# Twice as many softmax tiles turned by the DMA crossbar, v tiles kept, and small softmax operations written another way

## The chip, the cores and the metric

The kernel runs on 1 core of one Trainium2 chip. The metric is the device time of one execution in microseconds (us). Before the change three runs took 913.06, 915.95 and 915.98 us; the median is 915.95 us. The core has five instruction queues: PE (matrix products; its weight loads are listed as PEld), DVE, ACT and POOL (elementwise work), and SP, which in this kernel issues nearly all DMAs. Each queue runs its instructions in the order in which they were written into it; an instruction that waits holds back all that stand behind it on its queue.

## The reference

Eight batches of 576 tokens go through attention with 8 heads of 64 columns and then through a gated feed-forward layer. Scores below the row's maximum minus `tau` are left out of the softmax:

```python
scores = scale * np.matmul(q, k.transpose(0, 1, 3, 2))
thresh = np.max(scores, axis=-1, keepdims=True) - tau
scores = np.where(scores >= thresh, scores, -1000000000.0)
scores = scores - np.max(scores, axis=-1, keepdims=True)
attn = np.exp(scores)
attn = attn / (np.sum(attn, axis=-1, keepdims=True) + 1e-09)
attn_out = np.matmul(attn, v)
x = attn_out.transpose(0, 2, 1, 3).reshape(B, S, H * D)       # 8 x 576 x 512
h = np.maximum(x @ w_in, 0.0)                                 # 512 -> 1024
conv_out[:, s] = sum(conv_w[k] * hp[:, s + k] for k in (0, 1, 2))   # hp: h with a zero row at both ends
gate = 1.0 / (1.0 + np.exp(-conv_out))
out = h * gate @ w_out                                        # 1024 -> 512
```

## The kernel before

**Tiling.** Heads are handled two at a time; a batch has 4 such pairs of heads. The 576 query rows are five tiles: four of 128 rows and one of 64. A batch is cut into two chunks, tiles 0 and 1, and tiles 2, 3 and 4. A *pair* (numbered `i`, 64 in all) is one pair of heads in one chunk; a *unit* (numbered `u`, 160 in all) is one tile of one pair, with both heads. In a pair of even place `p` the tiles run upward, in one of odd place downward.

**One unit** (function `unit`, from line 552). For each head PE writes 128x576 scores into a PSUM buffer `ps_s` (two buffers; line 573 for batch 0, line 580 for the others). DVE takes the row's negative maximum (`top`, L588) into a column of a small tile `few`; ACT writes exp(score - maximum) into `em` (L597); the limit, maximum minus tau, is a small operation of its own for each head (L592 on ACT or L594 on DVE or POOL); DVE zeroes what lies below the limit and sums the row (`mask`, L600). Then, for both heads at once, a guard is added to the sums (L617), a second column is set to 1/576 in rows whose sum is zero (L621, the "empty row" operation), and the guarded sum is inverted (L624, DVE). POOL multiplies `em` by the inverse and adds that second column (`norm`, L633), 128x576 for each head.

**Turning a unit.** The product with `v` needs `em` with keys on the partitions. Mostly PE does that: nine 128x128 transposes of a full tile (L692), in two groups of four and one block that is turned with the pair's other tiles at the pair's end; ACT copies them from PSUM into `eT` (L687). From batch 1 on, the first full tile of a pair of even place goes another way (`crossed`, `cross`): ACT and POOL copy the upper and lower halfwords of `em` into `parts` (L326, L328), SP writes `parts` to a DRAM buffer `rows` (L665), and two transposing DMAs of the crossbar read that into `eT` (L670). `CROSS = (1, 0)` says: one tile in pairs of even place, none in those of odd place. That is 28 of 160 units.

**Attention product.** `attend` multiplies `eT` with `v` (L747, L756) for two pairs together, so it waits for both pairs' `eT`; ACT and DVE then write the chunk's activations `x`. `eT` has two buffers, one for each of the two pairs.

**Feed-forward.** `mm1` (L784, result `ph`) and `mm2` (L842, result `po`) of an earlier chunk are spread between the units. Between them stand `relu` into `hp` (L799), two taps (L806), tanh (L813), gate (L811) and the split into a high and a low part (L821, L333). `hp` gets a zero column at its left or right end by POOL (L794, L796).

**What sets the order.** `Plan.op` records every operation with an estimated duration; `Plan.run` is a list scheduler that walks through these estimates once, when the program is built, and thereby fixes each queue's order. For a DMA it keeps a clock of the transfers (`ring`) and adds `late` to what it believes the landing to take. Some operations may be put on another engine when their own has a backlog (`other=`).

## Time and profile before

| | before |
|---|---|
| runs shown | 913.06, 915.95, 915.98 us |
| span of the profiled execution | 910.8 us |
| PE busy | 874.6 us, 96% |
| DVE busy | 751.2 us, 82% |
| ACT busy | 673.8 us, 74% |
| POOL busy | 603.5 us, 66% |
| packets of the DMA queue that SP fills | 133.90 MB, 55.3% of 16 DMA engines |

The profile is one execution, seen by the hardware's own recorder. The span runs from the first to the last recorded instruction, 910.8 us; the median of the runs is 5.15 us above it. "Busy" is the time in which an engine had an instruction of the program in work. PE's matmuls overlap in its pipeline, so that the duration of one matmul is longer than the time after which the next one starts; where PE's work is priced, the distance from start to start is what counts.

### The profile page before, as it was taken

The page shows a single profiled execution, that of the slowest core. Times are in us where ns is not written, and L with a number is a line of the kernel's source. Part 1 is how long each engine was busy: PE and PEld are TensorE (multiplying, and loading weights), DVE is VectorE, ACT ScalarE, POOL GpSimd, SP SyncE. Part 2 cuts the span into 40 slices and gives each one's busy share as a digit, 9 for nine tenths or more (in the row PEclk, how much of TensorE's full clock was granted, in tenths as well). Part 3 has the DMA queues.
Part 4 walks back from the last instruction along what each step waited for, and adds up shares of the span by engine and source line. Part 5 has one row for each costly group of instructions (what it writes and reads, how often), then busy time and mean ns, then how long its engine had stood idle before and what let it go on. Part 6 is the DMA issues. An engine that isn't in the chain of part 4 may idle for free.

```text
span 910.8 us, 19147 instructions
## 1 busy us (share of the span) xinstructions
PE 874.6 (96%) x6056; PEld 708.6 (78%) x6056; DVE 751.2 (82%) x1871; ACT 673.8 (74%) x1459; POOL 603.5 (66%) x1027
## 2 busy tenths in 40 slices
PE   5978799999999999999999999999999999999998
PEld 3545577878878788888788797887888878887896
DVE  5988999988988689987889789996988779997542
ACT  4878687878777777777768687877867778776642
POOL 2656778875767677685767767776776758675322
PEclk9989899999999999999999999999999999999999
DMA  6555257667764667647665377557667276654000
GB/s 213 155 162 170 57 143 197 149 178 181 198 175 113 163 175 198 158 116 202 169 157 157 117 201 191 140 118 202 173 176 179 89 187 159 181 137 112 13 24 35
DMA packets 148260, 137.02 MB, mean 150 GB/s; under 512 B 85312, under 2 KB 116288, under 8 KB 148160
## 3 DMA queue, kind: packets, MB, share of 16 engines
q1 hardware_dynamic: 147296, 133.90, 55.3%
q10 hardware_dynamic: 864, 1.90, 0.6%
q8 instruction: 49, 0.80, 0.4%
q14 instruction: 51, 0.42, 0.2%
HBM read 58.88 MB, written 25.95 MB: 93 GB/s over the span
## 4 chain that ended last, share of the span: by engine, by line
PE 73%; ACT 8%; DVE 6%; POOL 5%; DMA 4%; issue 3%; SPq 2%; ACTq 0%; POOLq 0%; DVEq 0%
PE po L842 20%; PE ph L784 16%; PE pa L756 12%; PE ps_s L580 11%; PE ps_t L692 9%; PE ps_s L573 3%; ACT em L597 2%; POOL em L633 2%; DVE em L600 2%; ACT eT L687 2%; PE pa L747 2%; DVE few L588 2%; DMA q<-in_qd_dram 1%; SPq L513 1%; DMA q<-q 1%
## 5 line engine op out<-in xcount | busy, mean ns | idle before, releaser
L633 POOL TENSOR_SCALAR em<-em,few 128x576 f32<-128x576 f32 x287 | 262.8, 924 | 29.9 <-DVE few L624 22.1
L600 DVE SCALAR_TENSOR_TENSOR em<-ps_s,few,em 128x576 f32<-128x576 f32 x288 | 230.5, 812 | 25.4 <-ACT em L597 17.1
L588 DVE TENSOR_REDUCE few<-ps_s 128x1 f32<-128x576 f32 x288 | 211.5, 748 | 39.3 <-PE ps_s L573 22.0
L597 ACT ACTIVATE em<-ps_s,few 128x576 f32<-128x576 f32 x288 | 210.5, 741 | 35.8 <-DVE few L588 31.5
L784 PE MATMUL ph<-x,w1h 128*128 128x322 f32 (+1 forms) x1024 | 233.7, 304 | 0.6 <-ACT hp L799 0.5
L687 ACT ACTIVATE eT<-ps_t 128x512 f32<-128x512 f32 (+2 forms) x360 | 168.0, 487 | 24.5 <-PE ps_t L692 22.4
L784 PEld LDWEIGHTS ph<-x,w1h 128*128 128x128 f32 x1024 | 173.1, 189 | 4.7 <-issue 3.0
L692 PE MATMUL ps_t<-ident,em 128*128 128x128 f32 x1060 | 157.8, 280 | 6.5 <-POOL em L633 5.1
L580 PE MATMUL ps_s<-ks,q 128*128 128x288 f32 x896 | 156.8, 306 | 5.3 <-DMA q<-q 2.1
L784 PE MATMUL ph<-x,w1l 128*128 128x322 f32 (+1 forms) x512 | 151.3, 295 | 0.0
L692 PEld LDWEIGHTS ps_t<-ident,em 128*128 128x128 f32 x1060 | 126.5, 143 | 31.5 <-POOL em L633 14.9
L580 PEld LDWEIGHTS ps_s<-ks,q 128*128 128x128 f32 x896 | 129.2, 189 | 20.2 <-issue 8.2
L333 POOL TENSOR_TENSOR gl<-t,gh 128x255 fp32r<-128x255 f32 (+9 forms) x192 | 119.6, 637 | 28.5 <-ACT gh L821 27.5
L756 PE MATMUL pa<-eT,v 128*64 128x320 f32 (+1 forms) x1024 | 132.1, 410 | 0.0
L842 PE MATMUL po<-w2h,gh 128*128 128x512 f32 x288 | 117.9, 409 | 0.3 <-ACT hp L799 0.3
L756 PEld LDWEIGHTS pa<-eT,v 128*64 128x64 f32 x1024 | 70.4, 137 | 59.3 <-issue 15.8
L842 PE MATMUL po<-w2l,gh 128*128 128x512 f32 x288 | 113.3, 393 | 0.0
L842 PE MATMUL po<-w2h,gl 128*128 128x512 f32 x288 | 113.1, 393 | 0.1
L806 DVE SCALAR_TENSOR_TENSOR t<-hp,cr 128x321 f32<-128x321 f32 (+1 forms) x128 | 75.6, 594 | 28.0 <-ACT hp L799 28.0
L784 PEld LDWEIGHTS ph<-x,w1l 128*128 128x128 f32 x512 | 96.8, 189 | 0.2
L813 ACT ACTIVATE t<-t,cm 128x321 f32<-128x321 f32 (+1 forms) x128 | 68.0, 535 | 25.2 <-DVE t L806 12.2
L811 DVE SCALAR_TENSOR_TENSOR t<-t,hp 128x321 f32<-128x321 f32 (+1 forms) x128 | 73.1, 573 | 11.4 <-ACT t L813 9.8
(80 smaller groups left out, 1104.1 us busy)
## 6 DMA issues: line engine op xcount, KB each, us to landing
q<-q SPq DMA_DIRECT2D x336, 64.0 KB, 2.1
v<-in_vc_dram SPq DMA_DIRECT2D x64, 288.0 KB, 3.8
rows<-parts SPq DMA_DIRECT2D x28, 576.0 KB, 3.3
k<-in_kp_dram SPq DMA_DIRECT2D x35, 320.0 KB, 3.5
out_dram<-ot SPq DMA_DIRECT2D x36, 256.0 KB, 2.3
xk<-in_kt_dram SPq DMA_DIRECT2D x28, 288.0 KB, 3.4
ks<-xk SPq DMA_DIRECT2D x56, 144.0 KB, 3.3
xq<-in_qt_dram SPq DMA_DIRECT2D x56, 128.0 KB, 2.9
```

Source lines behind the costliest of these rows:

```text
L333: engines[e].tensor_tensor(dst, x, y, op=ALU.subtract)
L580: nc.tensor.matmul(ps[:, c, :CH], lhsT=q[:, h, o:o + n], rhs=k[:, h, c * CH:(c + 1) * CH], start=(i == 0), stop=(i == 1))
L588: nc.vector.tensor_reduce(few[:rows, nm], ps[:rows, :, :CH], op=ALU.max, axis=mybir.AxisListType.XY, negate=True)
L597: nc.scalar.activation(view(), ps[:rows, :, :CH], AF.Exp, bias=few[:rows, nm])
L600: nc.vector.scalar_tensor_tensor(view(), ps[:rows, :, :CH], few[:rows, th], view(), op0=ALU.is_ge, op1=ALU.mult, accum_out=few[:rows, total])
L633: engines[e].tensor_scalar(sl, sl, by, to, op0=ALU.mult, op1=ALU.add)
L687: "act", act(w, True), lambda dst=dst, src=src: nc.scalar.activation(dst(), src(pt), AF.Copy),
L692: nc.tensor.transpose(out=pt[:, at:at + P], in_=em[:, int(b * P):int(b * P) + P], identity=ident[:])
L756: nc.tensor.matmul(pa[j * D:(j + 1) * D, :w], lhsT=vt[:, blk, :], rhs=eT[:, :w // D, blk, :], start=False, stop=(r == 3))
L784: nc.tensor.matmul(ph[:, :an], lhsT=w1[w][:, cb, fs], rhs=xs[cb][:, h, :an], start=(cb == 0 and i == 0), stop=(cb == NCB - 1 and i == 2))
L806: nc.vector.scalar_tensor_tensor(t[:, :kn], hp[:, k:kn + k], cr[:, j, f:f + 1], y, op0=ALU.mult, op1=ALU.add)
L842: nc.tensor.matmul(po[:], lhsT=x[:, f, at:at + P], rhs=w[:, f, :], start=(f == 0 and i == 0), stop=(f == NFB - 1 and i == 2))
```

## The change

Seven things change, and with them the order on every queue.

- `CROSS` becomes `(1, 1)`: in pairs of odd place too, the first full tile goes by the crossbar. 56 units instead of 28.
- A pair of a batch's second chunk uses the `v` tile that the same heads loaded for the first chunk, from batch 1 on; there are four buffers for `v` instead of two. 36 loads instead of 64. `parts` has one buffer instead of two.
- `few` is four lasting tiles. They are filled once with a tiny number (2^-80 times 576), and two columns are set to `tau`, so that a maximum stands beside a `tau` and a sum beside the tiny number. The limits of both heads are then one DVE sum over pairs of columns (line 608 of the new kernel), and the guarded sums another (line 635). Both heads' masks come after that one limit.
- There is no empty-row operation. `norm` adds 2^-80 to each element and multiplies by the inverse: one column of `few` is read instead of two.
- `hp` is three lasting tiles whose zero columns are written once; the column that the first tap starts from is shifted instead.
- The limit and the guard can no longer go to POOL or ACT, and `norm` no longer to ACT.
- The planner's estimates of DMA times, of `norm` and of tanh are changed.

```diff
+LEAST = 2.0 ** -80
+FEW = 4
+VB = 4
-CROSS = (1, 0)
+CROSS = (1, 1)
...
-            self.tile = self.pool.tile(self.shape, self.dtype, tag=self.tag, bufs=self.bufs, name=self.name)
+            self.tile = self.home or self.pool.tile(self.shape, self.dtype, tag=self.tag, bufs=self.bufs, name=self.name)
...
+    fews = [const(f"few{i}", [P, 12], F32) for i in range(FEW)]
+    hps = [const(f"hp{i}", [P, CW + 2], F32) for i in range(HPB)]
+    for x in fews:
+        op("pool", 100, lambda x=x: nc.gpsimd.memset(x[:], LEAST * S), w=[(x, 0)], ahead=200.0)
+        op(
+            "dve", 150, lambda x=x: nc.vector.tensor_scalar(x[:, 1:4:2], x[:, 1:4:2], 0.0, tau_sb[:], op0=ALU.mult, op1=ALU.add),
+            w=[(x, 0)], r=[(tau_sb, 0)], ahead=100.0
+        )
+    for x in hps:
+        op("pool", 100, lambda x=x: nc.gpsimd.memset(x[:, 0:CW + 2:CW + 1], 0.0), w=[(x, 0)], ahead=5.0)
...
-        op(queue, issue, fn, ring=rows * (n * 0.225 + 4) * 0.0737, **kw)
+        op(queue, issue, fn, ring=rows * n * 0.0149, **kw)
...
-        vt = plan.buf(wk, "v", 2, [P, NBLK, D], F32, f"v_{i}")
+        if b and chunks[pairs[i][0]].new[0]:
+            return vts[i - NP]
+        vt = plan.buf(wk, "v", VB, [P, NBLK, D], F32, f"v_{i}")
...
+            def limit():
+                pairs = few[:rows, :2 * m].rearrange("p (h two) -> p h two", two=2)
+                nc.vector.tensor_reduce(few[:rows, 8:8 + m], pairs, negate=True, **add)
...
-            op("dve", 125, limit, w=[(few, ("th", h))], r=[(few, ("nm", h)), (ntau, 0)], ahead=a, other=[("pool", 260), ("act", 110)])
-            op("dve", 738, mask, w=[(em, h), (few, ("sum", h))], r=[(ps, 0), (few, ("th", h))], ahead=a)
+            late.append(mask)
+            if h == m - 1:
+                op("dve", 85, limit, w=[(few, "th")], r=[(few, ("nm", x)) for x in range(m)], ahead=a)
+        for h in range(m):
+            op("dve", 738, late[h], w=[(em, h), (few, ("sum", h))], r=[(pss[h], 0), (few, "th")], ahead=a)
...
-            engines[e].tensor_scalar(few[:rows, inverse], few[:rows, sums], 1e-9, 1.0, op0=ALU.add, op1=ALU.mult)
-        def even(e):
-            engines[e].tensor_scalar(few[:rows, shift], few[:rows, sums], 0.0, 1.0 / S, op0=ALU.is_equal, op1=ALU.mult)
+        def guard():
+            pairs = few[:rows, 4:4 + 2 * m].rearrange("p (h two) -> p h two", two=2)
+            nc.vector.tensor_reduce(few[:rows, inverse], pairs, **add)
...
-                    engines[e].tensor_scalar(sl, sl, by, to, op0=ALU.mult, op1=ALU.add)
+                engines[e].tensor_scalar(sl, sl, LEAST, few[:rows, 10 + h:11 + h], op0=ALU.add, op1=ALU.mult)
-            choice = {"pool": 807, "dve": 400, "act": 625}
+            choice = {"pool": 728, "dve": 400}
...
-        parts = plan.buf(wk, "parts", 2, [P, 2, 2 * S], U16, f"parts_{u}")
+        parts = plan.buf(wk, "parts", 1, [P, 2, 2 * S], U16, f"parts_{u}")
-            w=[(rows, 0)], r=[(parts, 0), (parts, 1)], ahead=a, late=-500
+            w=[(rows, 0)], r=[(parts, 0), (parts, 1)], ahead=a, late=350
-            op("sp", 1560, turn, w=[(eT, (off, j))], r=[(rows, 0)], ahead=a, late=100, ring=1785)
+            op("sp", 1560, turn, w=[(eT, (off, j))], r=[(rows, 0)], ahead=a, late=350, ring=1840)
...
-        def edge():
-            if o:
-                nc.gpsimd.memset(hp[:, 0:1], 0.0)
-            if k0 + kn == S:
-                nc.gpsimd.memset(hp[:, kn + 1:kn + 2], 0.0)
-            nc.scalar.activation(hp[:, o:o + an], ph[:, :an], AF.Relu, scale=0.5)
+            nc.scalar.activation(hp[:, 1:1 + an], ph[:, :an], AF.Relu, scale=0.5)
```

What the queues hold now is shown at three places around pairs 24 and 25, the first two pairs of batch 3 (units 60 and 61, and 62 and 63). In a name such as `ps_t_62_0_4515`, 62 is the unit, 0 the group of blocks, and the last number only counts what was written before.

**PE, the turning of pair 25.** Before, unit 62 is turned by two groups of four transposes, between feed-forward matmuls (`ph`):

```order
L784 MATMUL ph_4_6_4502<-x_16_3236,w1h_275 128x256
L784 MATMUL ph_4_6_4502<-x_17_3253,w1h_275 128x256
L784 MATMUL ph_4_6_4502<-x_17_3253,w1l_301 128x256
L784 MATMUL ph_4_6_4502<-x_17_3253,w1h_275 128x256
L692 MATMUL ps_t_62_0_4515<-ident_83,em_62_4309 128x128 x4
L692 MATMUL ps_t_62_4_4522<-ident_83,em_62_4309 128x128 x4
L784 MATMUL ph_4_6_4502<-x_18_3497,w1h_275 128x256
L784 MATMUL ph_4_6_4502<-x_18_3497,w1l_301 128x256
L784 MATMUL ph_4_6_4502<-x_18_3497,w1h_275 128x256
```

In the changed kernel no transpose of unit 62 is left; at the pair's end only unit 63 is turned, and its last block alone (before, that last group held a block of unit 62 as well):

```order
L701 MATMUL ps_t_63_0_4279<-ident_100,em_63_4186 128x128 x4
L701 MATMUL ps_t_63_4_4288<-ident_100,em_63_4186 128x128 x4
L845 MATMUL po_9_4250<-w2h_765,gh_1021 128x512
L845 MATMUL po_9_4250<-w2h_765,gl_1026 128x512
L845 MATMUL po_9_4250<-w2l_787,gh_1021 128x512
L701 MATMUL ps_t_63_8_4302<-ident_100,em_63_4186 128x128
```

Nine transposes are gone from this pair, and so from each of the 28 pairs of odd place from batch 1 on.

**PE, ahead of the attention product of pairs 24 and 25, in the changed kernel.** These rows stand between the second crossbar instruction that writes `eT` of pair 25 and the product that reads it (in the program's order over all queues):

```order
L596 MATMUL ps_s_66_0_4368<-ks_3_3_4063,q1_27_4169 128x288
L596 MATMUL ps_s_66_0_4368<-ks_3_3_4063,q2_27_4177 128x288
L596 MATMUL ps_s_66_0_4368<-ks_3_3_4063,q1_27_4169 128x288
L596 MATMUL ps_s_66_0_4368<-ks_3_3_4063,q2_27_4177 128x288
L596 MATMUL ps_s_66_1_4376<-ks_3_3_4063,q1_27_4169 128x288
L596 MATMUL ps_s_66_1_4376<-ks_3_3_4063,q2_27_4177 128x288
L596 MATMUL ps_s_66_1_4376<-ks_3_3_4063,q1_27_4169 128x288
L596 MATMUL ps_s_66_1_4376<-ks_3_3_4063,q2_27_4177 128x288
L756 MATMUL pa_24_4389<-eT_24_4153,v_24_3825 64x256 x2
L756 MATMUL pa_25_4392<-eT_25_4297,v_25_3865 64x256 x2
L765 MATMUL pa_24_4389<-eT_24_4153,v_24_3825 64x256 x8
L765 MATMUL pa_25_4392<-eT_25_4297,v_25_3865 64x256 x8
```

Eight score matmuls of unit 66 are all that PE is given there.

**SP, the crossbar of pairs 24 and 25.** Before, one pair goes by the crossbar, and both load `v` (`q1`, `q2` and `ks` are operands of the scores, moved between partitions; `xq` and `k` are loads):

```order
L513 DMA q1_27_4375<-q1_27_4375 64x256
L513 DMA q2_26_4377<-q2_26_4377 64x256
L549 DMA v_24_4447<-in_vc_dram 128x576
L670 DMA_TRANSPOSE eT_24_4457<-rows_60_4299 128x9x128 x2
L549 DMA v_25_4507<-in_vc_dram 128x576
L513 DMA ks_3_3_4369<-xk_3_3_4245 64x576
L513 DMA q1_27_4375<-q1_27_4375 64x256
L513 DMA q2_27_4437<-q2_27_4437 64x256 x2
L538 DMA xq_28_4567<-in_qt_dram 128x256
L492 DMA k_28_4579<-in_kp_dram 128x640
```

Now a second write of `rows` and a second pair of transposing DMAs stand within the next dozen issues; the loads of `v` that remain are those of the first chunk's pairs (26 and 27 here):

```order
L679 DMA_TRANSPOSE eT_24_4153<-rows_60_4030 128x9x128 x2
L562 DMA v_26_4204<-in_vc_dram 128x576
L524 DMA q1_27_4169<-q1_27_4169 64x256 x2
L524 DMA q2_27_4177<-q2_27_4177 64x256
L674 DMA rows_62_4238<-parts_62_4217 128x2304
L524 DMA q2_27_4177<-q2_27_4177 64x256
L562 DMA v_27_4256<-in_vc_dram 128x576
L549 DMA xq_29_4265<-in_qt_dram 128x256
L524 DMA q1_27_4169<-q1_27_4169 64x256
L503 DMA k_29_4277<-in_kp_dram 128x640
L524 DMA q2_27_4177<-q2_27_4177 64x256
L679 DMA_TRANSPOSE eT_25_4297<-rows_62_4238 128x9x128 x2
```

Pair 25's crossbar has moved into the stretch in which the operands of pairs 27 and 28 are being fetched.

**DVE, the softmax of unit 62.** Before, the first head's mask can stand right behind the second head's maximum, and limit, guard and empty-row operations are TENSOR_SCALARs, some of them on POOL (here the first head's limit):

```order
L624 RECIPROCAL few_61_4224<-few_61_4224 128x2
L588 TENSOR_REDUCE few_62_4290<-ps_s_62_1_4293 128x1
L600 SCALAR_TENSOR_TENSOR em_62_4309,few_62_4290<-ps_s_62_0_4274,few_62_4290,em_62_4309 128x576
L594 TENSOR_SCALAR few_62_4290<-few_62_4290,ntau_113 128x1
L806 SCALAR_TENSOR_TENSOR t_4_1_4335<-hp_4_1_3856,cr_512 128x255
L600 SCALAR_TENSOR_TENSOR em_62_4309,few_62_4290<-ps_s_62_1_4293,few_62_4290,em_62_4309 128x576
L806 SCALAR_TENSOR_TENSOR t_4_1_4335<-hp_4_1_3856,cr_512,t_4_1_4335 128x255
L617 TENSOR_SCALAR few_62_4290<-few_62_4290 128x2
L621 TENSOR_SCALAR few_62_4290<-few_62_4290 128x2
L624 RECIPROCAL few_62_4290<-few_62_4290 128x2
```

Now both maxima come first, then one limit for both heads, then both masks:

```order
L604 TENSOR_REDUCE few2_85<-ps_s_62_0_4078 128x1
L604 TENSOR_REDUCE few2_85<-ps_s_62_1_4088 128x1
L809 SCALAR_TENSOR_TENSOR t_4_3_4119<-hp2_98,cr_462 128x255
L608 TENSOR_REDUCE few2_85<-few2_85 128x2
L809 SCALAR_TENSOR_TENSOR t_4_4_4127<-hp0_91,cr_462 128x255
L775 TENSOR_TENSOR x_22_3555<-pa_22_4096,x_22_3555 128x320
L614 SCALAR_TENSOR_TENSOR em_62_4114,few2_85<-ps_s_62_0_4078,few2_85,em_62_4114 128x576
L614 SCALAR_TENSOR_TENSOR em_62_4114,few2_85<-ps_s_62_1_4088,few2_85,em_62_4114 128x576
L809 SCALAR_TENSOR_TENSOR t_4_3_4119<-hp2_98,cr_462,t_4_3_4119 128x255
L775 TENSOR_TENSOR x_23_3557<-pa_23_4099,x_23_3557 128x320
L635 TENSOR_REDUCE few2_85<-few2_85 128x2
L604 TENSOR_REDUCE few3_87<-ps_s_63_0_4146 128x1
```

The limit now follows both maxima, the first head's mask follows the limit, and limit and guard are TENSOR_REDUCEs on DVE alone.

48 lines of the change are left out of this document (19 added, 29 removed).

## The prediction

> **What bounds the kernel now.** I read the page's sums first, then the chain that ended last, then the busy time by stage.
>
> ```profile
> span 910.8 us, 19147 instructions
> PE 874.6 (96%) x6056; PEld 708.6 (78%) x6056; DVE 751.2 (82%) x1871; ACT 673.8 (74%) x1459; POOL 603.5 (66%) x1027
> PE 73%; ACT 8%; DVE 6%; POOL 5%; DMA 4%; issue 3%; SPq 2%; ACTq 0%; POOLq 0%; DVEq 0%
> core 0: us, PE busy (x) PEld busy (x) DVE busy (x) ACT busy (x) POOL busy (x), PEclk, DMA share, GB/s
> 0.00:137.00 137.00, 113.28 (x669) 70.39 (x670) 115.12 (x276) 101.68 (x209) 83.03 (x134) 0.95 0.49 151
> 137.00:865.00 728.00, 719.34 (x5170) 601.32 (x5169) 618.86 (x1567) 555.30 (x1213) 509.23 (x871) 1.00 0.61 158
> 865.00:910.80 45.80, 42.01 (x221) 36.93 (x219) 17.24 (x31) 16.80 (x39) 11.27 (x22) 1.00 0.08 29
> ```
>
> PE is busy 96% of the span and makes 73% of the last chain. The three stages say more: the first 137 us are batch 0 and the preparation of the weights, where PE idles 137.00 - 113.28 = 23.7 us and DVE is as busy as PE; in the middle 728 us PE idles 728.00 - 719.34 = 8.7 us and DVE still has 15% free; the last 46 us are feed-forward alone. So in the middle, where the crossbar is used, a microsecond taken from PE's work is a microsecond of time as long as PE's inputs come early enough. What PE waited for, in the first stage and in the middle:
>
> ```profile
> PE ps_s L573 <- DVE em L600: 9.0, 4, 4.6
> PE ps_s L573 <- ACT q L503: 6.4, 1, 6.4
> PE ps_s L580 <- DMA q<-q: 2.1, 1, 2.1
> PE ps_t L692 <- POOL em L633: 1.3, 3, 0.7
> ```
>
> The first two rows are of the first stage (a score buffer not yet released by the mask; the first load), the other two are the largest of the middle. None is an `eT` from the crossbar.
>
> **The transposes that go.** 28 pairs lose nine transposes each, 252 in all. PE's own timeline gives their price from start to start:
>
> ```profile
> 361.41 0.39 PE L842 MATMUL po<-w2h,gl 128*128 128x512 f32 x1
> 361.64 0.40 PE L842 MATMUL po<-w2l,gh 128*128 128x512 f32 x1
> ...
> 363.12 0.70 PE L580 MATMUL ps_s<-ks,q 128*128 128x288 f32 x4
> 363.65 1.04 PE L692 MATMUL ps_t<-ident,em 128*128 128x128 f32 x8
> 364.45 0.40 PE L784 MATMUL ph<-x,w1h 128*128 128x322 f32 x1
> ...
> 366.09 0.31 PE L784 MATMUL ph<-x,w1h 128*128 128x322 f32 x1
> 366.24 0.31 PE L784 MATMUL ph<-x,w1l 128*128 128x322 f32 x1
> ```
>
> Eight transposes begin at 363.65 and the next product at 364.45: 0.80 us, 0.10 us each. 252 x 0.10 = **25.2 us less** work on PE, all of it in the stage where PE has no room. In the same way a `po` matmul costs 0.23 us, a `ph` matmul 0.15 us, a score matmul 0.53 / 4 = 0.13 us.
>
> What stands in their place lies beside PE:
>
> ```profile
> L326 ACT ACTIVATE parts<-em x28: 1151/1164/1199, 134.5 to 827.0; 128x1152 uint16<-128x1152 uint16 x28
> L328 POOL COPY parts<-em x28: 1132/1143/1445, 135.1 to 826.9; 128x1152 uint16<-128x1152 uint16 x28
> L687 ACT ACTIVATE eT<-ps_t 128x512 f32<-128x512 f32 x232 | 134.7, 600 | 22.0 <-PE ps_t L692 21.0
> L687 ACT ACTIVATE eT<-ps_t 128x256 f32<-128x256 f32 x36 | 13.9, 387 | 1.6 <-PE ps_t L692 1.4
> L687 ACT ACTIVATE eT<-ps_t 128x128 f32<-128x128 f32 x28 | 8.2, 291 | 0.0
> ```
>
> ACT gets one copy of 1.16 us for each new crossed tile and loses two evacuations of 0.60 us; a third shrinks from 0.39 to 0.29 us: about 0.13 us less for each, 4 us in all. POOL gets 28 x 1.14 = 32 us. Neither is near its limit (555 and 509 of 728 us). If that cover were gone, each copy would hold back what stands behind it on its queue by its 1.2 us.
>
> [...]
>
> **The new wait.** DMAs, their issue on SP, and one crossbar from issue to use:
>
> ```profile
> rows<-parts SPq DMA_DIRECT2D x28, 576.0 KB, 3.3
> v<-in_vc_dram SPq DMA_DIRECT2D x64, 288.0 KB, 3.8
> L670 SPq DMA_TRANSPOSE eT<-rows x56: 1257/1561/3349, 141.8 to 836.8; - x56
> DMA to landing us min/median/max: 3.6/4.3/6.5
> 141.78 2.75 SPq L670 DMA_TRANSPOSE eT<-rows  x2
> 153.32 0.66 PE L747 MATMUL pa<-eT,v 64*64 64x256 f32 x8
> SPq L850 <- ACT ot L849: 91.2, 16, 24.2
> ```
>
> The first crossing's second DMA is issued at about 143.2, lands some 4.3 us later, and the product that reads it starts at 153.3: some 6 us to spare. That is because a pair of even place has the whole odd pair between itself and their joint product. A tile of the odd pair has not. I counted, in the changed program's order, what PE is given between a pair's second crossbar instruction and the product, at the prices above (transposes 0.10, `ph` scaled by its columns): for the 28 even pairs 9.6 to 25.8 us, for the 28 odd ones **1.1 to 10.2 us**, the middle one about 5.3. Pair 25, shown above, has eight score matmuls, 8 x 0.13 = 1.1 us. Where that work is shorter than the landing, PE waits the rest: with 4.3 us, seven of the 28 fall short, by 9 us together; with 5 us it is some 14; with the longest landing seen, 6.5 us, 39 us. Zero is the other end, if SP runs ahead of PE. I take **10 us more**, near the median landing.
>
> SP itself gets 56 x 1.56 = 87 us more of crossbar issue, 28 more issues of `rows`, and 28 issues of `v` less. It has room on average (one kind of wait alone, for an output tile, is 91 us long); where it hasn't, the operands of the scores stand behind a crossbar issue of up to 3.3 us, and PE's 2.1 us wait above is of that kind. The transfers grow by 28 x 576 KB for `rows`, as much again, from the code's shapes, for what the crossbar reads and writes, less 28 x 288 KB for `v`: some 24 MB on 137 MB, so I estimate the DMA share of the middle stage at 0.61 x 1.2 = 0.73. I put no price on that beyond the ends of the wait.
>
> **The small operations.** Limits, guards, empty rows, inverses, zero columns and the normalisation before (durations in ns, least / median / most):
>
> ```profile
> L594 DVE TENSOR_SCALAR few<-few,ntau x170: 195/207/216, 8.6 to 842.6; 128x1 f32<-128x1 f32 x170
> L594 POOL TENSOR_SCALAR few<-few,ntau x89: 257/265/789, 9.8 to 844.5; 128x1 f32<-128x1 f32 x89
> L617 POOL TENSOR_SCALAR few<-few x91: 191/299/569, 11.5 to 834.1; 128x2 f32<-128x2 f32 x77, 128x1 f32<-128x1 f32 x14
> L617 DVE TENSOR_SCALAR few<-few x69: 139/169/1390, 16.0 to 845.7; 128x2 f32<-128x2 f32 x51, 128x1 f32<-128x1 f32 x18
> L621 DVE TENSOR_SCALAR few<-few x93: 135/156/467, 16.1 to 820.3; 128x2 f32<-128x2 f32 x79, 128x1 f32<-128x1 f32 x14
> L621 POOL TENSOR_SCALAR few<-few x67: 214/226/587, 11.8 to 845.7; 128x2 f32<-128x2 f32 x49, 128x1 f32<-128x1 f32 x18
> L624 DVE RECIPROCAL few<-few x160: 144/159/168, 12.7 to 845.9; 128x2 f32<-128x2 f32 x128, 128x1 f32<-128x1 f32 x32
> L600 DVE DVE_READ_ACCUMULATOR em<-ps_s,few,em 128x1 f32 x288 | 23.5, 82 | 0.0
> L796 POOL MEMSET hp<- 128x1 f32 x64 | 6.0, 97 | 36.2 <-DVE t L811 35.1 <-DVE few L594 0.5
> L633 POOL TENSOR_SCALAR em<-em,few x287: 812/824/1739, 13.0 to 847.0; 128x576 f32<-128x576 f32 x144
> ```
>
> At the medians DVE loses 170 x 0.207 + 69 x 0.169 + 93 x 0.156 = 61 us and POOL 89 x 0.265 + 91 x 0.299 + 67 x 0.226 = 66 us, with the zero columns (6 us for those at the right end) and the 35 us for which POOL's queue stood still before those. DVE gains 160 + 160 sums over two pairs. No such sum is in the trace; between the accumulator's read, 82 ns, and the limit, 207 ns, I take the RECIPROCAL's 159 ns, which works on the same tile: 51 us, so DVE ends 10 us lower (35 lower to 5 higher by the ends). [...] The new `norm` reads one column less; I leave it at 0.82 us.
>
> None of this is PE's work, so in the middle it is worth only what PE waits for these engines: at most the 8.7 us of idle time there. I take **4 us less**, half (nothing and 8.7 are the ends): while PE waits for a late `eT`, its other inputs catch up too. In the first stage I take another **4 us less** of the 9.0 us of waits for masks (nothing and 9.0 are the ends), since DVE is as busy as PE there, and limits no longer cross over to POOL and back. The lasting tiles are filled in the idle time before the first scores. The granted clock, 0.95 in the first stage, cost at most 7 us of PE there; I leave it.
>
> **Sum.** -25.2 + 10 - 4 - 4 = -23.2 us. Against the profiled execution that is a span of 887.6 us; the median of the runs lies 5.15 us above the span before, so **893 us**, 2.5% faster.
>
> **Rivals.** (1) *The crossbar lands in time.* SP runs ahead of PE, the planner's new estimates (`late` 350 instead of -500 and 100) keep its promises, and the wait term is nothing, with up to all the idle time of the middle gone: -25.2 - 4 - 4 to -25.2 - 9 - 8.7, 873 to 883 us. For it: no wait of the middle before was for a crossing. Against it: seven of the 28 odd pairs have less PE work than the landing takes.
>
> (2) *Score buffers are held too long.* The first head's mask now waits for the second head's maximum and the limit, some 0.75 + 0.16 us, and both buffers are held. If one in four of the 112 full units of the middle stage made PE wait 0.9 us, that is 25 us, and the gain is gone: 905 to 918 us. Against it: PE's waits for the mask in the middle are smaller than the two rows quoted, and DVE has 15% free.
>
> (3) *Slower: the crossbar is late everywhere.* With twice the crossings the second DMA lands later. The point from which it decides is a landing of about 6 us instead of 4.3: then the shortages of the 28 odd pairs add to 29 us. At 6.5 us, the most seen, they add to 39 us, and with the queue's delay of the scores' operands, 2.1 us at a few places, the sum is -25.2 + 39 + 6 = +20: up to 936 us, from 919. For it: DMA share and SP's issue time rise together, and `parts` has one buffer. Against it: 56 landings before have a median near their least value, 3.6. [...]
>
> That the planner's order doesn't do what the change says I exclude: the rows of the order show the transposes gone.
>
> **Chances.** The forecast, 884 to 904 us: 50%. Rival 1: 25%. Rival 2: 13%, of it 8 below 913.2, 4 within 0.3% and 1 above. Rival 3: 12%. Differences under 0.3% (2.7 us) can't be told from no change. So faster 0.83, same 0.04, slower 0.13. The range leaves out most of rival 3, and little at the lower end: 876 to 913 us.
>
> **What would show it.** PE's transposes drop from 1060 to 808; PE busy in the middle stage falls by about 25 us. A list of PE's waits with `pa` waiting for DMA `eT<-rows`, on odd pairs, some 10 us, shows the second term; none shows rival 1. Waits of PE's scores for DVE's masks would show rival 2; crossbar landings of 6 us rival 3. The prediction is wrong if PE's idle time in the middle stage grows by more than 25 us.

## The result, and the profile after

Four runs of the changed kernel took 924.1, 928.57, 933.14 and 938.57 us, median 930.86; the kernel before took 914.7 us beside them. The slowest of the four, 938.57 us, counts as a slow run and is left out of the ratio. That ratio is 1.0148, with a 95% interval of 1.0108 to 1.0188: 1.5% slower, where 2.5% faster was forecast. From the page of the profiled execution after, the busy times, the chain and two groups:

```profile
span 931.4 us, 18212 instructions
PE 862.3 (93%) x5804; PEld 686.5 (74%) x5804; DVE 763.1 (82%) x1862; ACT 667.8 (72%) x1401; POOL 532.4 (57%) x688
PE 56%; DMA 13%; ACT 9%; DVE 7%; SPq 6%; POOL 4%; issue 4%; ACTq 0%; POOLq 0%; DVEq 0%
L701 PE MATMUL ps_t<-ident,em 128*128 128x128 f32 x808 | 124.1, 280 | 19.7 <-ACT eT L696 8.7
L809 DVE SCALAR_TENSOR_TENSOR t<-hp,cr 128x321 f32<-128x321 f32 (+1 forms) x128 | 92.1, 722 | 19.3 <-ACT hp L803 17.8
```

The transposes are gone (808 instead of 1060), but PE makes only 56% of the last chain, where it made 73%. The stretches of the kernel after, cut as before (the last stage begins at 885 us), with the same columns:

```profile
0.00:137.00 137.00, 104.04 (x602) 63.93 (x603) 110.34 (x269) 91.89 (x186) 60.00 (x85) 0.95 0.44 141
137.00:885.00 748.00, 716.54 (x4988) 585.96 (x4987) 636.14 (x1566) 559.27 (x1179) 461.77 (x590) 0.99 0.74 189
885.00:931.00 46.00, 41.71 (x217) 36.65 (x215) 16.66 (x30) 16.69 (x38) 10.57 (x14) 1.00 0.08 30
```

PE's idle time is 33.0 us in the first stage (23.7 before) and 748.00 - 716.54 = 31.5 us in the middle (8.7 before). PE's busy time fell by 12.3 us, its idle time rose by 32.9: together the 20.6 us by which the span grew. What PE waited for in the whole span after (us in total, times, longest; two rows left out):

```profile
PE ph L794 <- ACT hp L803: 10.5, 6, 3.8
PE ps_s L589 <- ACT q L514: 9.3, 1, 9.3
PE ps_t L701 <- ACT eT L696: 8.7, 10, 2.8
PE ps_t L701 <- POOL em L642: 6.4, 6, 1.9
PE ps_s L589 <- DVE em L614: 6.3, 5, 2.1
PE pa L756 <- ACT eT L696: 5.2, 4, 2.5
PE ps_s L596 <- DMA q<-q: 4.1, 6, 1.4
...
PE pa L756 <- DMA eT<-rows: 1.7, 2, 1.1
```

The wait that the prediction priced at 10 us, the product waiting for the crossbar's `eT`, is the last row: 1.7 us. The new waits are for ACT, POOL and DVE. Where the time is lost shows when I follow the 36 attention products (64x256 matmuls of `pa`) through both traces: the first begins at 22.3 us before and 26.8 after, the eighth at 131.4 and 145.3, the eleventh at 199.6 and 220.6, the last at 855.9 and 876.3. So 14 us are lost by the eighth, 21 by the eleventh, and from there to the end the distance stays about 20: in the batches that follow, what the missing transposes save is eaten up as it arises.

One of those waits from close by, first PE, then ACT of the kernel after on the timeline (start, us, engine, operation):

```profile
241.29 0.28 PE L794 MATMUL ph<-x,w1h 128*128 128x256 f32 x1
...
242.71 0.74 PE L596 MATMUL ps_s<-ks,q 128*128 128x288 f32 x4
247.25 0.38 PE L794 MATMUL ph<-x,w1h 128*128 128x256 f32 x1 [3.80 <-ACT hp L803]
...
249.13 2.12 PE L596 MATMUL ps_s<-ks,q 128*128 128x288 f32 x8
251.18 1.01 PE L756 MATMUL pa<-eT,v 64*64 64x320 f32 x8
```

```profile
242.32 1.22 ACT L696 ACTIVATE eT<-ps_t 128x512 f32<-128x512 f32 x4
...
244.74 0.40 ACT L824 ACTIVATE gh<-t 128x255 fp32r<-128x255 f32 x1
245.16 1.37 ACT L611 ACTIVATE em<-ps_s,few 128x576 f32<-128x576 f32 x2
246.42 0.50 ACT L816 ACTIVATE t<-t,cm 128x255 f32<-128x255 f32 x1
246.82 0.38 ACT L803 ACTIVATE hp<-ph 128x256 f32<-128x256 f32 x1
```

Next on PE's queue is a `ph` product, and its buffer is free only after ACT's relu at 246.82. The sums that this relu reads were done by 241.57 at the latest, when the last `ph` matmul ahead of the wait ended. In between ACT works through eleven other operations of its queue with no pause above 0.17 us: copies into `eT`, operands of the scores, a split, two exponentials and a tanh. So it isn't a late transfer that PE waits for here but ACT's queue, which has more to do just then than fits beside PE's work. Behind the wait the eight score matmuls take 2.05 us from start to start (249.13 to 251.18), 0.26 each, twice the 0.13 of before; the last section comes back to that.

### The profile page after: what moved, and what is told of

Its sections match the earlier page's. It is cut to its first block, busy times and chain, and to the rows that moved or that the text cites. A ratio compares the mean times of both kernels' runs of the same rounds, so it can differ in the third digit from the quotient of the medians.

```text
span 931.4 us, 18212 instructions
## 1 busy us (share of the span) xinstructions
PE 862.3 (93%) x5804; PEld 686.5 (74%) x5804; DVE 763.1 (82%) x1862; ACT 667.8 (72%) x1401; POOL 532.4 (57%) x688
## 4 chain that ended last, share of the span: by engine, by line
PE 56%; DMA 13%; ACT 9%; DVE 7%; SPq 6%; POOL 4%; issue 4%; ACTq 0%; POOLq 0%; DVEq 0%
PE po L845 14%; PE ph L794 13%; PE pa L765 9%; PE ps_s L596 8%; PE ps_t L701 6%; DMA q<-q 4%; DMA q<-in_qd_dram 3%; DMA xk<-in_kt_dram 3%; PE ps_s L589 3%; SPq L524 2%; POOL em L642 2%; SPq L679 2%; PE pa L756 2%; ACT em L611 2%; DVE em L614 2%
## 5 line engine op out<-in xcount | busy, mean ns | idle before, releaser
L642 POOL TENSOR_SCALAR em<-em,few 128x576 f32<-128x576 f32 x288 | 240.2, 845 | 172.0 <-DVE few L638 165.1
L604 DVE TENSOR_REDUCE few<-ps_s 128x1 f32<-128x576 f32 x288 | 210.1, 748 | 43.8 <-PE ps_s L596 27.2
L614 DVE SCALAR_TENSOR_TENSOR em<-ps_s,few,em 128x576 f32<-128x576 f32 x288 | 225.9, 811 | 21.9 <-ACT em L611 14.8
L611 ACT ACTIVATE em<-ps_s,few 128x576 f32<-128x576 f32 x288 | 207.7, 741 | 46.9 <-DVE few L604 43.0
L344 POOL TENSOR_TENSOR gl<-t,gh 128x255 fp32r<-128x255 f32 (+9 forms) x192 | 123.8, 657 | 117.4 <-ACT gh L824 115.6
L596 PEld LDWEIGHTS ps_s<-ks,q 128*128 128x128 f32 x896 | 129.7, 190 | 26.9 <-issue 10.5
L696 ACT ACTIVATE eT<-ps_t 128x512 f32<-128x512 f32 (+3 forms) x304 | 132.0, 455 | 22.2 <-PE ps_t L701 20.1
L701 PE MATMUL ps_t<-ident,em 128*128 128x128 f32 x808 | 124.1, 280 | 19.7 <-ACT eT L696 8.7
L701 PEld LDWEIGHTS ps_t<-ident,em 128*128 128x128 f32 x808 | 96.4, 143 | 43.8 <-issue 17.1
L809 DVE SCALAR_TENSOR_TENSOR t<-hp,cr 128x321 f32<-128x321 f32 (+1 forms) x128 | 92.1, 722 | 19.3 <-ACT hp L803 17.8
L809 DVE SCALAR_TENSOR_TENSOR t<-hp,cr,t 128x321 f32<-128x321 f32 (+1 forms) x128 | 86.8, 683 | 0.3
L814 DVE SCALAR_TENSOR_TENSOR t<-t,hp 128x321 f32<-128x321 f32 (+1 forms) x128 | 78.1, 614 | 8.5 <-ACT t L816 7.9
```

The lines of the kernel that those rows point to most:

```text
L344: engines[e].tensor_tensor(dst, x, y, op=ALU.subtract)
L596: nc.tensor.matmul(ps[:, c, :CH], lhsT=q[:, h, o:o + n], rhs=k[:, h, c * CH:(c + 1) * CH], start=(i == 0), stop=(i == 1))
L604: nc.vector.tensor_reduce(few[:rows, nm], ps[:rows, :, :CH], op=ALU.max, axis=mybir.AxisListType.XY, negate=True)
L611: nc.scalar.activation(view(), ps[:rows, :, :CH], AF.Exp, bias=few[:rows, nm])
L614: nc.vector.scalar_tensor_tensor(view(), ps[:rows, :, :CH], few[:rows, th], view(), op0=ALU.is_ge, op1=ALU.mult, accum_out=few[:rows, total])
L642: engines[e].tensor_scalar(sl, sl, LEAST, few[:rows, 10 + h:11 + h], op0=ALU.add, op1=ALU.mult)
```

## The experiments

In the table "after" is the changed kernel and "before" the one before. "Median" is of the runs, "ratio" that to the kernel before, run beside each, with its interval. Idle time of PE is from the profiled execution, up to 137 us and from there to the last 46 us, which are feed-forward alone.

| run | median us | ratio | idle before / after 137 us | transposes |
|---|---|---|---|---|
| the kernel before | 914.7 | 1 | 23.7 / 8.7 | 1060 |
| the kernel after | 930.86 | 1.0148 (1.0108 to 1.0188) | 33.0 / 31.5 | 808 |
| e1, after, odd pairs not crossed | 938.07 | 1.0235 (1.0184 to 1.0285) | 33.7 / 18.3 | 1060 |
| e2, after, loads of v paced | 934.71 | 1.0214 (1.0183 to 1.0245) | 33.2 / 34.4 | 808 |
| e3, after, old estimates of DMAs | 921.18 | 1.0080 (1.0051 to 1.0110) | 27.2 / 25.6 | 808 |
| e4, before, odd pairs crossed | 928.13 | 1.0136 (1.0100 to 1.0172) | 25.3 / 31.1 | 808 |
| e5, small operations alone | 921.54 | 1.0067 (1.0050 to 1.0084) | 28.7 / 8.9 | 1060 |
| e6, v kept alone | 919.72 | 1.0050 (1.0030 to 1.0070) | 28.6 / 9.0 | 1060 |
| e7, after, shuffled | 934.9 | 1.0213 (1.0165 to 1.0260) | 32.5 / 31.8 | 808 |
| e8, before, shuffled | 911.52 | 0.9971 (0.9952 to 0.9990) | 21.4 / 9.6 | 1060 |
| e9, crossing that nothing reads | 928.5 | 1.0174 (1.0144 to 1.0203) | 24.2 / 15.2 | 1060 |
| e10, e4 with a later product | 936.31 | 1.0251 (1.0220 to 1.0283) | 25.5 / 39.6 | 808 |
| e11, e5 with a limit for each head | 911.87 | 0.9983 (0.9959 to 1.0007) | 21.8 / 7.9 | 1060 |
| e12, e9, copies alone | 924.03 | 1.0109 (1.0089 to 1.0128) | 25.4 / 13.8 | 1060 |
| e13, e9, DMAs alone | 923.3 | 1.0089 (1.0073 to 1.0105) | 26.9 / 13.1 | 1060 |
| e14, before, no crossing | 939.3 | 1.0269 (1.0253 to 1.0286) | 25.5 / 8.7 | 1312 |
| e15, e11, no crossing | 937.43 | 1.0240 (1.0211 to 1.0269) | 23.0 / 9.6 | 1312 |
| e16, e4 with an early source | 947.72 | 1.0358 (1.0335 to 1.0382) | 25.6 / 46.7 | 808 |
| e17, before, two crossed in even pairs | 944.98 | 1.0333 (1.0303 to 1.0363) | 24.5 / 45.7 | 808 |
| e18, e11, two crossed in even pairs | 908.85 | 0.9922 (0.9895 to 0.9949) | 25.0 / 21.5 | 808 |

### How much the order alone does: e7 and e8

One latency in the planner's estimates is changed by 2 ns, in both kernels, so that the list comes out in another order with the same operations.

```diff
-LATENCY = {"pe": 210.0, ...
+LATENCY = {"pe": 212.0, ...
```

> The changed kernel with one number of the planner, the believed delay from PE to another engine, at 212 instead of 210 ns: no instruction is added or removed, only the order moves. Theory L (the time hangs on how well an order happens to fit, and the order of before was a good one among many): the time moves by 5 us or more either way. Rival (the time is set by the work and the waits that the change makes): it stays within 4 us of 931.

> The kernel before with the same number at 212 instead of 210 ns. Theory L: the time rises by 5 to 15 us, with no other change at all. Rival: it stays within 4 us of 915.

The kernel before moved by -0.3%, the kernel after by +0.65%; the eighth attention product moved from 131.4 to 127.2 us and from 145.3 to 147.8. With one other order of each the 1.5% are unlikely to be luck of the order, but a difference of some 0.7% between two kernels can be; the single parts below are read with that in mind.

### The parts alone: e1, e4, e5, e6, e3, e2

The crossing taken out of the change, and put alone into the kernel before:

```diff
-CROSS = (1, 1)      # e1, in the kernel after
+CROSS = (1, 0)
-CROSS = (1, 0)      # e4, in the kernel before
+CROSS = (1, 1)
```

> The changed kernel with CROSS back at (1, 0), all else as changed. Theory Q (the doubled crossbar costs in the middle, by what it does to the queue of SP, about what its transposes save): PE idles less than 15 us after 137 us instead of 31.5, the transposes are back with some 25 us, and the time stays near the changed kernel's 931 (922 to 938). Rival S (all is lost at the start, the crossbar's saving in the middle is whole): the time rises by some 20 us, to 948 or more. Both expect the first attention product to stay late, at 26 to 27 us instead of 22.

> The kernel before with CROSS = (1, 1) alone. Theory Q: the transposes fall to 808, but PE's idle time after 137 us grows by 15 us or more and the time is 905 to 922. If the crossbar's saving is whole (rival S): 886 to 894. The first attention product stays at 22 us by both.

Alone, the crossing removes the 252 transposes and still makes the kernel 1.4% slower, with 31.1 us of idle time after 137 us. In the changed kernel, taking it back makes things a little worse (1.0235). So the effects don't add, and the crossing isn't the only loss. The stretches of e1 (up to 137 us, and from there to the last 46 us; columns as above):

```profile
0.00:137.00 137.00, 103.29 (x595) 63.27 (x596) 108.24 (x266) 90.38 (x183) 59.24 (x83) 0.94 0.43 139
137.00:892.00 755.00, 736.75 (x5238) 612.92 (x5237) 626.25 (x1566) 560.54 (x1209) 431.11 (x563) 0.99 0.54 144
```

e1 splits the loss of the changed kernel. Its span is 938.4 us: everything but the second crossing costs 27.6 us. With the crossing it is 931.4, 7.0 us less: PE's busy time falls by 20.6 us (882.9 to 862.3), and its idle time in the middle rises by 13.2 (18.3 to 31.5). The 7 us are near what another order moves (0.65% is 6 us); the 27.6 are not.

The small operations alone (the kernel after without the second crossing, with `v` loaded again, two buffers for `parts` and the old estimates of DMAs), and `v` kept alone in the kernel before (with one buffer for `parts`, as in the change):

```diff
-CROSS = (1, 1)      # e5, in the kernel after
+CROSS = (1, 0)
-        if b and chunks[pairs[i][0]].new[0]:
-            return vts[i - NP]
-VB = 4
+VB = 2
...
+        if b and chunks[pairs[i][0]].new[0]:      # e6, in the kernel before
+            return vts[i - NP]
-        vt = plan.buf(wk, "v", 2, ...
+        vt = plan.buf(wk, "v", 4, ...
```

> The changed kernel with CROSS at (1, 0), v loaded each time, two parts buffers and the estimates of DMA times of before: what is left of the change is the softmax's small operations, the lasting tiles of hp and few, and the estimates of norm and tanh. Theory D (they make the start late and cost in the middle): 922 or more. Rival (they are beside PE's work and harmless or useful): 906 to 917, start as before.

> The kernel before with v kept alone (four buffers, one parts buffer). Theory S: the first attention product is 2 to 5 us later than 22.3 and the time 917 to 925, since the loads that are saved later lie beside other work. Rival: the loads of v are hidden anyway, at the start too, and the time stays at 912 to 917.

Each costs some 0.5 to 0.7%, all of it in the first stage (28.7 and 28.6 us of idle time instead of 23.7, the eighth product at 141.2 and 137.7 us instead of 131.4); in the middle neither adds to it (8.9 and 9.0 us of idle time). That `v` is loaded 28 times less saves nothing: those loads were hidden.

The estimates of the DMAs put back as they were, in the kernel after (e3), and the first batch's loads of `v` tied to the product of two pairs earlier (e2):

```diff
-        op(queue, issue, fn, ring=rows * n * 0.0149, **kw)      # e3
+        op(queue, issue, fn, ring=rows * (n * 0.225 + 4) * 0.0737, **kw)
-            ... late=350            # rows
+            ... late=-500
-            ... late=350, ring=1840     # turn
+            ... late=100, ring=1785
...
+            r=[(xs[pairs[i - 2][0]][pairs[i - 2][1]], 0)] if not b and i > 1 else ()      # e2, load of v
```

> The changed kernel with the planner's DMA estimates of before (the transfer time of a load, `late` -500 and 100, 1785 ns for a crossbar transfer). Theory E (the new, shorter transfer times let the planner put loads and what waits for them too early, at the start above all): the first attention product is back at 22 to 23 us instead of 26.8, the eighth at 131 to 138 instead of 145, and the time falls to 915 to 924. Rival D (the softmax's new order makes the start late): only the first product comes back, and the time stays at 926 or more.

> The changed kernel with the loads of v in batch 0 ordered as if v had two buffers (a load only after the attention product of two pairs earlier). Theory S (four buffers let two loads of v go ahead of what the start needs): the first attention product is back at 22 to 24 us, the eighth at 131 to 136 instead of 145, and the time falls by 6 to 12 us, to 919 to 925. Rival D (the new order of the softmax operations makes the start late): the first product gains 3 us, the eighth stays later than 140, and the time stays within 4 us of 931.

The old estimates win back 0.7% of the 1.5; the eighth product is at 135.9 us instead of 145.3. Pacing the loads of `v` wins nothing. Part of this is seen at the start. SP and ACT in the first 10 us after:

```profile
2.85 5.21 SPq L562 DMA_DIRECT2D v<-in_vc_dram  x4
3.92 4.89 ACTq L385 DMA_DIRECT2D stage<-in_w_in_dram  x3
8.86 1.03 ACT L514 ACTIVATE q<-q 128x256 f32<-128x256 f32 x3 [5.69 <-DMA q<-in_qd_dram]
```

and before:

```profile
2.90 1.48 SPq L549 DMA_DIRECT2D v<-in_vc_dram  x2
3.90 2.04 ACTq L374 DMA_DIRECT2D stage<-in_w_in_dram  x3
5.98 0.72 ACT L503 ACTIVATE q<-q 128x256 f32<-128x256 f32 x2 [2.82 <-DMA q<-in_qd_dram]
```

The same three issues on ACT's queue take 4.89 us instead of 2.04 while SP issues four loads instead of two, and `q` is scaled 2.9 us later, which is the row of 9.3 us in PE's waits. In e2 two loads of `v` and two of `xq` stood there and the three issues took as long (4.88 us); in e3 and e6, with two loads of `v`, they took 2.49 and 2.28.

### The masks that wait for both heads: e11

e5, with a sum for each head instead of one for both:

```diff
-            def limit():
-                pairs = few[:rows, :2 * m].rearrange("p (h two) -> p h two", two=2)
-                nc.vector.tensor_reduce(few[:rows, 8:8 + m], pairs, negate=True, **add)
+            def limit(h=h, th=th):
+                nc.vector.tensor_reduce(few[:rows, th], few[:rows, 2 * h:2 * h + 2], negate=True, **add)
-            late.append(mask)
-            if h == m - 1: ...
-        for h in range(m): ...
+            op("dve", 85, limit, w=[(few, ("th", h))], r=[(few, ("nm", h))], ahead=a)
+            op("dve", 738, mask, w=[(em, h), (few, ("sum", h))], r=[(ps, 0), (few, ("th", h))], ahead=a)
```

> The small operations alone (921.5 us, 1.0067, 28.7 us of idle time before 137 us), with a limit for each head, a DVE sum over the two columns of that head alone, so that the first head's mask no longer waits for the second head's maximum; 142 more such sums on DVE, 0.145 us each, 21 us on DVE in all. Theory that the first stage is lost because both score buffers are held for one common limit (the second rival of the prediction): idle time before 137 us goes back to about 24 us and the time to 915 to 917 us (1.000 to 1.003). Rival, that the loss comes with the new transfer order or the shifted engine shares at the start: idle time before 137 us stays at 28 to 30 us, the time at 920 to 925 us (1.005 to 1.011).

The loss is gone: idle time of the first stage 21.8 us instead of 28.7, the eighth product at 132.8 us instead of 141.2, the time 0.8% shorter than e5, though DVE has 128 sums more. The ratio difference is near what a shuffle gives; the 8.4 us at the eighth product are twice the 4.2 and 2.5 us that the shuffles moved it. PE's waits of the first stage, two rows of e5 and then of e11:

```profile
PE ps_s L587 <- DVE em L612: 5.7, 5, 2.1
PE pa L754 <- ACT eT L694: 5.3, 4, 2.5
```

```profile
PE ps_s L587 <- DVE em L611: 4.6, 5, 1.4
PE pa L750 <- ACT eT L690: 1.2, 2, 0.9
```

The common limit is what costs, but not in the way of the second rival, which had PE waiting for masks: those waits are 5.7 us with it, 4.6 without, and 9.0 in the kernel before. What grows are waits for ACT: for its copies into `eT` (5.3 us against 1.2) and for one relu (2.5 us, none in e11). How a limit on DVE comes to delay ACT's queue was not followed.

### What the crossing costs: e9, e12, e13

The kernel before, with the odd pairs' tiles crossed into a tile that nothing reads, and then the two halves of that work by themselves (`parts` has one buffer in all three; in e9 no copy waits for it):

```diff
+    shadow = const("shadow", [P, 2, NBLK, D], F32)
...
             transposes(now, ems, len(tiles), eT)
+            if p % 2 and not plain(b) and t == [x for x in tiles if TILES[x][1] == P][0]:
+                cross(now, em, shadow, 0)                  # e9
+                cross(now, em, shadow, 0, moves=False)     # e12: copies into parts alone
+                cross(now, em, shadow, 0, copies=False)    # e13: rows written from a weight tile, and turned
```

> The kernel before, in which the first full tile of the odd pairs is copied, written to DRAM and turned by the crossbar as in the crossing alone, but into a tile that nothing reads; PE keeps all its 1060 transposes, and parts has one buffer. It holds the traffic of the new crossings without anything that waits for them. Theory of the traffic (the copies on ACT and POOL, the crossbar's issue on SP and the DMA packets hold up the queues on which PE depends): PE idles 25 us or more after 137 us as in the crossing alone (31.1), at 1060 transposes, so the time is 930 us or more (1.02 and up). Theory of the late eT (the product that reads eT of an odd pair waits, and the in-order queues of ACT and DVE stand behind it): PE's idle time after 137 us stays at 9 to 13 us, the time is 914 to 920 us (1.000 to 1.006).

> The crossing that nothing reads (1.0174), without its DMAs: the kernel before with the 56 copies into parts alone added on ACT and POOL (28 x 1.17 and 28 x 1.14 us), all transposes kept. If the copies hold up PE (an evacuation, a norm or a relu stands behind a copy of 1.2 us): 922 to 930 us (1.010 to 1.018). If the DMAs do: 913 to 918 us (1.000 to 1.005).

> The crossing that nothing reads, without its copies: the kernel before with the 28 writes to DRAM (of the same size, from a tile that lies ready) and the 56 transposing DMAs alone added, all transposes kept. If the DMAs hold up PE (SP's queue is held 87 us longer, the DMA share rises by a quarter): 922 to 930 us (1.010 to 1.018), with more of PE's waits for operands that SP moves. If the copies do: 913 to 918 us (1.000 to 1.005).

A crossing that nobody waits for costs 1.7%, 15.6 us of span; its copies alone 1.1%, its DMAs alone 0.9%. Both halves cost, and e9's idle time after 137 us (15.2 us) explains 6.5 of its 15.6 us. Most of the rest stands in PE's busy time, 883.5 us instead of 874.6 with the same matmuls. They don't run longer (a `ph` matmul 302 ns in the mean, 301 before; a `po` matmul 401, 398 before), but `ph` and `po` together take 8.2 us more from start to start, idle time left out. I read these as waits too short to show as idle: in the kernel before, the `po` matmul at 361.41 us lasts 0.39 us and the next starts 0.23 us after it, so by that row a wait of up to 0.16 us, an estimate, would lie under the matmul ahead. No run took that apart. The theory of the traffic had 25 us of idle time and 930 us, and is too high. The theory of the late `eT` said 1.000 to 1.006 for e9 and falls here as the only cause.

### Lateness, or no other work: e10, e16, e17

e10 lets the planner believe the landing to be 2.5 us later; e16 lets the crossbar of an odd pair read the rows of the even pair ahead, so that it can run earlier (its `eT` then holds another tile's values); e17 crosses two tiles in even pairs, which have a whole odd pair of slack, and none in odd ones.

```diff
-            op("sp", 1560, turn, ... r=[(rows, 0)], ahead=a, late=100, ring=1785)
+            op("sp", 1560, turn, ... r=[(rows, 0)], ahead=a, late=2600, ring=1785)     # e10, in e4
+        source = kept.get("rows", rows) if crossings[0] % 2 else rows                  # e16, in e4
+            op("sp", 1560, turn, ... r=[(source, 0)], ahead=a, late=100, ring=1785)
-CROSS = (1, 0)
+CROSS = (2, 0)                                                                        # e17, in the kernel before
```

> The crossing alone (928.1 us, 1.0136, 31.1 us of idle time after 137 us), in which the planner believes the landing of the two transposing DMAs to come 2.5 us later (late 2600 instead of 100), so that PE is given other work ahead of the product that reads them. Theory of the late eT: the waits shrink, the idle time after 137 us falls to some 10 to 18 us, with it the half clock, and the time to 910 to 918 us (0.995 to 1.003). Theory of the traffic: idle time of 25 us or more is left, 924 us or more (1.009 and up).

> The crossing alone (1.0136, 31.1 us of idle time after 137 us, 808 transposes), in which the crossbar of an odd pair reads the DRAM rows of the even pair ahead of it, so that its eT can land some microseconds earlier; the odd pair's own tile is still copied and written to DRAM, but nothing reads it, so eT holds another tile's values there. Number of transposes, copies, writes and crossbar DMAs are those of the crossing alone. Theory of lateness: what remains is the traffic, some 926 - 25 = 901 us of span, a ratio of 0.985 to 0.995, with 10 to 17 us of idle time after 137 us. Theory that PE lacks the transposes as filler: time and idle time stay, 1.009 to 1.016, 25 us and more.

> The kernel before with two tiles crossed in pairs of even place and none in those of odd place: as many crossings as in the change (56), 504 transposes less than with none, and every crossed tile has a whole odd pair ahead of its product. Theory of lateness: the traffic costs 15 us and the transposes save 25, so 900 to 908 us (0.984 to 0.993). Theory that the number of crossings decides, wherever they stand: 924 us and more (1.010 and up).

All three are slower than e4, and e16 is slower than either theory had it. More slack doesn't help; it leaves 40 to 47 us of idle time. Lateness is there in e4: three products, at 450, 558 and 795 us, start or go on 0.14 us after a crossing's landing, and PE stands 6.5 us before them (one of these waits, 3.8 us, is listed under a tanh). In e10 and e16 no such wait is left, and both are slower. What PE waits for in e17, whole span:

```profile
PE ps_t L692 <- POOL em L633: 16.8, 19, 2.4
PE ps_s L580 <- DVE em L600: 9.2, 9, 3.1
PE ps_s L573 <- DVE em L600: 9.2, 5, 4.6
PE ph L784 <- ACT hp L799: 8.2, 6, 3.3
...
PE pa L747 <- DMA eT<-rows: 4.3, 1, 4.3
```

Normalised tiles from POOL, masks from DVE, relu from ACT; one wait for a crossing. In e16 the two largest after 137 us are relu from ACT (14.6 us) and normalised tiles from POOL (13.6 us). I read this so: with nine transposes of so many tiles gone, PE reaches the next units before the softmax has made them.

### Where crossing pays: e14, e15, e18

No crossing at all, in the kernel before and in e11; and two crossed tiles in even pairs in e11:

```diff
-CROSS = (1, 0)
+CROSS = (0, 0)      # e14 in the kernel before, e15 in e11
-CROSS = (1, 0)
+CROSS = (2, 0)      # e18 in e11
```

> The kernel before with no crossing at all: PE gets the nine transposes of the 28 even pairs too, 252 x 0.10 = 25 us more work, and ACT and POOL, SP and the DMAs lose what the 28 crossings cost. If every crossing costs what the new ones do when nothing waits for them (15 us for 28): 910.8 + 25 - 15 = 921 us of span (about 1.011). If the first 28 cost nothing, because they had slack: 936 us (1.025 or more). If crossing costs more than it saves everywhere: below the kernel before (under 0.997).

> The small operations with a limit for each head (0.9983) with no crossing at all. By the same three readings relative to 0.9983: 1.010, 1.023 or more, under 0.995. A result that differs from the one of the kernel without crossings by more than 0.006 shows that the two parts don't add.

> The small operations with a limit for each head (0.9983), with two tiles crossed in pairs of even place. POOL has 90 us less to do here than in the kernel before, so the new copies find more room. Theory of lateness: 895 to 906 us (0.979 to 0.991), faster than both kernels. Theory of the number: 1.008 and up.

Read by the number of crossings, spans of the profiled executions:

| crossed tiles | small operations as before | on DVE, a limit for each head |
|---|---|---|
| 0 | 937.2 (e14) | 937.2 (e15) |
| 28 | 910.8 (before) | 910.4 (e11) |
| 56, two in even pairs | 941.9 (e17) | 907.2 (e18) |

The first 28 are worth their full 26 us in either form. The next 28, in even pairs, cost 31 us with the small operations as before and gain 3 with the new ones. The 3 us are within what another order moves; the 35 us between e17 and e18 are not. e18 is 0.8% faster than the kernel before, which is just beyond the shuffles, and faster than the changed kernel. From its views and those of e17 (busy times; POOL's norm and guard, PE's waits; first e17, then e18):

```profile
PE 868.2 (92%) x5804; PEld 686.0 (73%) x5804; DVE 768.6 (82%) x1877; ACT 676.6 (72%) x1409; POOL 625.7 (66%) x1043
L633 POOL TENSOR_SCALAR em<-em,few 128x576 f32<-128x576 f32 x287 | 258.4, 908 | 28.0 <-DVE few L624 22.0 <-DVE few L594 4.6 <-DMA q<-q 0.4
L617 POOL TENSOR_SCALAR few<-few 128x2 f32<-128x2 f32 (+1 forms) x92 | 26.5, 288 | 75.0 <-DVE em L600 71.8 <-DVE few L624 0.2
```

```profile
PE 857.2 (94%) x5804; PEld 679.8 (75%) x5804; DVE 760.6 (84%) x1990; ACT 663.6 (73%) x1373; POOL 529.2 (58%) x688
L636 POOL TENSOR_SCALAR em<-em,few 128x576 f32<-128x576 f32 x288 | 233.7, 821 | 204.2 <-DVE few L632 155.2 <-DVE few L605 42.3 <-DMA rows<-parts 1.9
PE ps_t L695 <- POOL em L636: 8.0, 9, 2.6
PE ps_s L594 <- DVE em L611: 4.4, 5, 2.7
PE ph L788 <- ACT hp L797: 1.7, 2, 1.4
```

In e17 POOL's queue stands 75.0 us in front of guards that mostly wait for a mask, with the copies and the next norms behind them, and a norm takes 908 ns. In e18 POOL does 529 us of work instead of 626, it is there before the norm's input (204 us of waiting in front of norms), a norm takes 821 ns, and PE's waits for POOL's norms, DVE's masks and ACT's relu are half or less. Which of the small operations does it wasn't tried one by one.

## Why the prediction was wrong, point by point

**The transposes: right in size.** PE's transposes take 111.1 us from start to start before and 85.7 after, idle time left out: 25.4 us less, against 25.2.

**The crossing: -15.2 us forecast (-25.2 + 10), -7.0 measured in the changed kernel (e1), +16.3 alone in the kernel before (e4).** The step that failed is "a microsecond taken from PE's work is a microsecond of time as long as PE's inputs come early enough", with only `eT` looked at among the inputs, and copies and transfers priced at nothing. In the whole change PE's busy time fell by 12.3 us instead of 25.2, and its idle time in the middle rose by 22.8 instead of 10 - 4 = 6. The copies and DMAs were to lie "beside PE" since "neither is near its limit (555 and 509 of 728 us)". The share of the DMA engines was estimated well (0.73; it is 0.74), only without a price. e12 and e13 priced both: some 10 and 8 us (1.1 and 0.9%) before anybody reads the result. And with the transposes gone PE stands at the end of the softmax of DVE, ACT and POOL; e16 and e17 show it with no late crossing and with one. A share of 70% (509 of 728 us) doesn't mean that an engine's result is there when needed. The group of POOL's guards in the kernel before shows it, 27 us of work and 78 us in which the whole queue stood in front of them, mostly for a mask:

```profile
L617 POOL TENSOR_SCALAR few<-few 128x2 f32<-128x2 f32 (+1 forms) x91 | 26.9, 296 | 77.6 <-DVE em L600 75.3 <-DVE few L624 0.2
```

**Everything else: -8 us forecast (-4 - 4), +27.6 measured (e1).** This is the larger miss, 35.6 us against 8.2 at the crossing; together they are the 43.8 us between the forecast span and the measured one. The two terms for the small operations and the first stage were taken from PE's waits for other engines, and the new order of the queues was taken to cost nothing. Of the 27.6 us, 10.0 are idle time of the first stage and 9.6 of the middle. The sign that the prediction set for itself, over 25 us more idle time in the middle, was not reached (22.8); it left out the first stage and the waits inside PE's busy time. The 5.15 us added between span and median compared different executions; within one, 933.14 us and a span of 931.4, it is 1.7.

**The new wait: wrong term.** 10 us were taken, 1.7 came. SP's crossbars landed in time (median 4.1 us, longest 5.9, against 4.3 and 6.5), as the first rival said; its time of 873 to 883 us didn't follow, as its other terms were the same. Lateness can cost (6.5 us in e4), but e10 and e16, where it is gone, are slower still.

**The first stage: wrong sign.** 4 us less were forecast; 14 were lost by the eighth product. A price of the common limit stood only in the second rival, for the middle stage and at 13%; e5 against e11 shows 8.4 us of it, in the first stage and with waits for ACT instead of masks. The planner's new estimates had been taken as a promise about landings; e3 shows that they cost 9.4 us by the eighth product, and e6 puts 6.3 on keeping `v`. These three overlap and were found in different surroundings; their sum isn't to be held against the 14.

**Small operations on DVE: the size was right, the total wasn't.** A sum over pairs of columns takes 148 ns at the median, 159 had been taken. But DVE rose by 12 us instead of falling by 10: the two taps and the gate rose from 229.7 to 257.0 us, 27 us more for the same elements. They were not in the sum at all. In e11 they take 245 us, in e4 246, so both parts of the change slow them. The traces show POOL's work beside them: of the 192 taps and gates of 255 columns, those with no POOL instruction at the same time took 412 to 486 ns before and 406 to 486 ns after; those with POOL at work for nine tenths of their time took 703 and 780 ns in the mean, up to 1.5 and 1.7 us. No run changed POOL's work alone. One of them after, POOL's operation above it:

```profile
242.51 1.42 POOL L344 TENSOR_TENSOR xk<-xk,ks 128x576 fp32r<-128x576 f32 x1 [1.65 <-ACT ks L536]
242.53 1.68 DVE L814 SCALAR_TENSOR_TENSOR t<-t,hp 128x255 f32<-128x255 f32 x1
```

The rows of the new sum and of the crossbar after:

```profile
L608 DVE TENSOR_REDUCE few<-few x160: 131/148/160, 12.5 to 865.1; 128x2 f32<-128x4 f32 x128, 128x1 f32<-128x2 f32 x32
L679 SPq DMA_TRANSPOSE eT<-rows x112: 1257/1472/2622, 147.9 to 871.1; - x112
DMA to landing us min/median/max: 3.5/4.1/5.9
```

**The third rival.** Its result, slower, came true; its mechanism, landings of 6 us, didn't; that the time fell into its range of 919 to 936 us is luck. Leaving all the turning to PE is no answer either: e14, with no crossing, is 2.7% slower than the kernel before. So the first 28 crossings gain, and the next 28, with the small operations as before, lose (1.4% in e4, 3.3% in e17).

**What stays open.** How the 27.6 us divide between the common limit, the estimates and `v`; which of the small operations makes the second 28 crossings bearable; whether the change's own place for the second crossing, one in odd pairs, would gain with a limit for each head (only two in even pairs was run); and what stretches ACT's issues at the start.
